# The last block's store: its copy split between VectorE and ScalarE, and one store half ahead of it moved to GpSimd's queue

## The chip, the cores and the metric

The kernel runs on one core of a Trainium2 chip. The metric is the device time of the run in microseconds (us), lower is better. Each time is a whole execution; a profiled execution also gives a span (first to last recorded instruction), which is a little shorter than its time.

## The reference

The program computes an attention with a 32-slot memory for 8 batches and 8 heads, and feeds its output, 4608 tokens of 512 columns, to a gated feed-forward layer (float32 in, float32 out):

```python
a = softmax(phi); k_m = a.T @ k; v_m = a.T @ v          # per batch and head
x = softmax(scale * q @ k_m.T) @ v_m                    # (8*576, 512)
g = x @ w_gate                                          # (4608, 1536)
out = (silu(g) * (x @ w_val)) @ w_out                   # (4608, 512)
```

What concerns us is the last line's last product, `h @ w_out`, and the way its results leave the chip.

## The kernel before

The kernel works batch by batch (8 batches of 576 tokens). The attention part is folded into two weight tiles per batch, so that a batch is 24 slots of gate and value matmuls (L508), a gate on ScalarE (L525), a multiplication on VectorE (L531), and then the output product. Instructions are written out in one fixed order by hand; each engine runs its own in that order, and the framework places the semaphores.

The output product is a 2x2 block scheme with seven products in place of eight: sums of blocks of `h` are formed ahead (POOL or VectorE, L553, L596, L657), and `products()` turns seven matmul groups (L719, PSUM tiles `p_os`, `p_oc`, `p_oa`) into four result blocks, called `c11`, `c22`, `c12` and `c21`. A batch has 576 tokens and the scheme takes 512 of them. The 64 tokens that are left over are gathered for four batches at a time: `products(b, ..., quad)` with `quad` 0 (batches 0 to 3) and `quad` 1 (batches 4 to 7) forms the same four blocks of 128 rows (two batches of 64) by 256 columns.

`quad` 1 is the end of the program, and its order is `c11` earlier, then `c22`, `c12`, `c21`. Each of them is made by `leftover(...)`:

- `c22` and `c12` add a PSUM result to a kept SBUF tile (VectorE, L788, tiles `t_p` and `t_q`);
- `c21` only copies its PSUM result to the SBUF tile `t_q` (on VectorE for the last quad: L332, called by the helper `copy`);
- the block then leaves in two DMAs of 64 rows by 256 columns, 64 KB each (L679, `store_leftover`). In the last quad the first half is issued by SP and, for all blocks but `c11`, the second half by ScalarE's queue.

`t_q` is one tile with two parts: `c12` writes part 1 and `c21` part 0. GpSimd's last computation before the end is a row of twelve block sums of the quad (L657 and L553, `quad_sums`).

After the last store, SP waits for all DMA semaphores, a few at a time, and all engines meet in two barriers (the rows of L1104).

Of the kernel before, what the change touches and what calls it, by code (L numbers as in the profile page):

```python
# [14 lines left out]
def kernel(  # L15
# [19 lines left out]
    nc = tc.nc  # L35
# [45 lines left out]
    def done(*tiles):  # L81

        for t in tiles:
            free.append(held.pop(id(t))[0])
# [243 lines left out]
    def copy(eng, out, in_):  # L328
        if eng == "a":
            nc.scalar.copy(out=out, in_=in_)  # L330
        else:
            nc.vector.tensor_copy(out=out, in_=in_)  # L332
# [344 lines left out]
    def store_leftover(t_o, b, cols, eng):  # L677

        eng.dma_start(out=out_b[b, 512:S, cols], in_=t_o)  # L679

    def products(b, by_hand, quad=None):

        h = DM // 2
# [3 lines left out]
        end = quad == 1 or (quad is None and b + 1 == B)  # L687
# [87 lines left out]
            both("o2", 256, slice(0, DM))  # L775

        def leftover(name, room, half, cols):
            engs = (nc.sync, nc.scalar if end and name != "c11" else nc.sync)

            def run():  # L780
                if room:
                    t = mine[room, "all"][:, half]
                else:
                    t = work.tile([128, h], FP32, tag="to", name="t_o")
                home = mine[dict(c11="a", c12="c").get(name, "s")]
                other = dict(c11="p1", c22="p5", c12="q6").get(name)
                if other:
                    nc.vector.tensor_tensor(  # L788
                        out=t, in0=home[:, 0], in1=mine[other][:, 0], op=ALU.add
                    )  # L790
                else:
                    copy("v" if end else "a", t, home[:, 0])
                if name != "c22":
                    done(home)
                for k in range(2):
                    x = 4 * quad + 2 * (name > "c20") + k
                    store_leftover(t[64 * k:64 * k + 64], x, cols, engs[k])

            return run
# [3 lines left out]
            c11=c11, c22=c22, c12=c12, c21=c21,  # L803
        )
        if quad is not None:
            ops.update(
                c11=leftover("c11", None, 0, lo), c12=leftover("c12", "q6", 1, hi),
                c22=leftover("c22", "p5", 1, hi), c21=leftover("c21", "q6", 0, lo),
            )
# [299 lines left out]
```

The softmax here doesn't subtract the row's maximum and nothing guards it: scores larger than these inputs give would overflow.

## Time and profile before

| | us |
|---|---|
| time, median of 4 runs (235.64 to 235.99) | 235.79 |
| time of the profiled execution | 235.84 |
| its span | 233.9 |
| busy PE | 224.4 (96%) |
| busy VectorE | 183.3 (78%) |
| busy ScalarE | 173.5 (74%) |
| busy GpSimd | 140.5 (60%) |

The profiled execution took 235.84 us, 1.94 us more than its span. The program is bound by TensorE as a whole, and the change touches only its last five microseconds, from the end of the matmuls on. There the times of single instructions (the timeline) matter, not the shares of the span. SPq and ACTq are the instruction queues of SyncE and ScalarE, whose rows are the issuing of DMAs and semaphore waits.

### The profile page before, as it was taken

What the parts mean: (1) busy time and instruction counts of PE and PEld (TensorE: products, weight loads), DVE (VectorE), ACT (ScalarE), POOL (GpSimd) and SP (SyncE); (2) the same over time, 40 slices, a digit from 0 to 9 for tenths busy, and PEclk for the clock granted to TensorE, in tenths of its full rate; (3) what the DMA queues carried; (4) which work ended last, traced back from release to release, by engine and by line L of the source; (5) the groups of instructions that cost most, each with busy time, mean ns of one, the idle gap of its engine ahead of it and who ended that gap; (6) DMA issues with size and microseconds to landing.
All of it is one profiled execution on the core that took longest, in us unless ns stands there. A gap on an engine that the chain in (4) does not pass through costs nothing.

```text
span 233.9 us, 7201 instructions
## 1 busy us (share of the span) xinstructions
PE 224.4 (96%) x2825; PEld 169.6 (73%) x2825; DVE 183.3 (78%) x421; ACT 173.5 (74%) x369; POOL 140.5 (60%) x190
## 2 busy tenths in 40 slices
PE   7997799999999999999999999999999999999992
PEld 2554466778887776878788787877788778878881
DVE  4056799999966698989797767989799879977632
ACT  2758798988547889968896658968897789677220
POOL 8422536998199059665966688465745484038390
PEclk9999999999999999999999999999999999999998
DMA  6999999999995992999199946995023602211224
GB/s 209 210 211 205 199 207 207 228 238 267 205 244 142 260 252 39 233 224 153 35 254 212 187 136 118 252 225 90 16 77 102 113 0 94 90 38 54 64 75 134
DMA packets 36610, 36.84 MB, mean 157 GB/s; under 512 B 14560, under 2 KB 30944, under 8 KB 36576
## 3 DMA queue, kind: packets, MB, share of 16 engines
q0 software_dynamic: 16272, 22.42, 51.5%
q1 hardware_dynamic: 19536, 13.18, 23.2%
q10 hardware_dynamic: 768, 0.79, 1.1%
q8 instruction: 22, 0.36, 0.6%
q14 instruction: 12, 0.10, 0.1%
HBM read 42.47 MB, written 9.44 MB: 222 GB/s over the span
## 4 chain that ended last, share of the span: by engine, by line
PE 86%; DMA 8%; POOL 2%; ACT 1%; issue 0%; DVE 0%; POOLq 0%
PE p_v L508 21%; PE p_g L508 21%; PE p_os L719 20%; PE p_oc L719 10%; DMA W<-in_moe_w_gate_dram 8%; PE p_u L465 5%; PE p_oa L719 5%; PE p_kv L230 2%; PE p_g L389 1%; POOL t_kv L99 1%; POOL t_kv L103 1%; PE p_q L376 0%; POOL t_q L108 0%; ACT t_qT L330 0%; PE p_kv L258 0%
## 5 line engine op out<-in xcount | busy, mean ns | idle before, releaser
L531 DVE TENSOR_TENSOR t_h<-t_sg,p_v 128x288 bf16<-128x288 bf16 x192 | 81.9, 451 | 17.3 <-PE p_v L508 7.1
L508 PEld LDWEIGHTS <-t_U 128*128 128x128 bf16 x768 | 73.5, 98 | 23.3 <-issue 3.8
L525 ACT ACTIVATE t_sg<-p_g 128x288 bf16<-128x288 f32 x192 | 74.0, 424 | 17.8 <-PE p_g L508 11.5
L508 PE MATMUL p_g<-t_A,t_U 128*128 128x288 bf16 x384 | 77.2, 287 | 0.5 <-ACT t_U L487 0.5
L508 PE MATMUL p_v<-t_A,t_U 128*128 128x288 bf16 x384 | 77.3, 286 | 0.0
L719 PEld LDWEIGHTS <-t_S 128*128 128x128 bf16 x384 | 37.4, 98 | 4.6 <-issue 0.2
L596 POOL TENSOR_TENSOR t_S<-t_h 128x512 bf16<-128x512 bf16 x17 | 19.6, 1154 | 32.6 <-DVE t_h L531 30.5
L719 PEld LDWEIGHTS <-t_h 128*128 128x128 bf16 x288 | 27.1, 98 | 8.6 <-issue 5.0
L485 ACT CAST t_U<-p_u 128x512 bf16<-128x512 f32 x53 | 28.0, 607 | 6.6 <-PE p_u L465 6.6
L719 PE MATMUL p_os<-t_T,t_S 128*128 128x256 bf16 x192 | 23.7, 273 | 0.0
L553 POOL TENSOR_TENSOR t_S<-t_S,t_h 128x512 bf16<-128x512 bf16 x17 | 19.6, 1154 | 1.3
L553 POOL TENSOR_TENSOR t_S<-t_h 128x512 bf16<-128x512 bf16 x16 | 18.4, 1151 | 0.0
L553 POOL TENSOR_TENSOR t_S<-t_h,t_S 128x512 bf16<-128x512 bf16 x16 | 18.4, 1150 | 0.0
L465 PE MATMUL p_u<-W,t_kT 64*32 64x512 bf16 (+1 forms) x416 | 15.8, 364 | 0.7 <-DMA W<-in_moe_w_gate_dram 0.7
L866 PE MATMUL p_warm<-bones 128*128 128x512 bf16 x44 | 13.7, 453 | 1.7 <-DVE bones L888 1.7
L719 PE MATMUL p_os<-t_T,t_h 128*128 128x256 bf16 x96 | 14.8, 274 | 0.0
L489 DVE CAST t_U<-p_u 128x512 bf16<-128x512 f32 x19 | 12.4, 683 | 1.9 <-PE p_u L465 1.9
L445 DVE TENSOR_TENSOR t_A<-t_E,t_lz 128x576 bf16<-128x576 bf16 x16 | 11.4, 739 | 0.7 <-ACT t_lz L421 0.7
L719 PE MATMUL p_oc<-t_T,t_S 128*128 128x256 bf16 x96 | 12.0, 273 | 0.0
L719 PE MATMUL p_oa<-WO,t_h 128*128 128x256 bf16 x96 | 11.8, 273 | 0.0
L719 PE MATMUL p_oc<-WO,t_S 128*128 128x256 bf16 x96 | 11.8, 273 | 0.1
L719 PE MATMUL p_os<-WO,t_h 128*128 128x256 bf16 x96 | 11.8, 273 | 0.0
(106 smaller groups left out, 308.7 us busy)
## 6 DMA issues: line engine op xcount, KB each, us to landing
out_dram<-t_o SPq DMA_DIRECT2D x15, 512.0 KB, 3.8
t_kv<-in_k_dram POOLq DMA_DIRECT2D x8, 576.0 KB, 10.2
t_q<-in_q_dram POOLq DMA_DIRECT2D x8, 576.0 KB, 8.7
t_kv<-in_v_dram POOLq DMA_DIRECT2D x8, 576.0 KB, 14.5
t_phi<-in_phi_dram POOLq DMA_DIRECT2D x6, 576.0 KB, 8.2
WO<-in_moe_w_out_dram POOLq DMA_DIRECT2D x3, 512.0 KB, 19.4
W<-in_moe_w_gate_dram POOLq DMA_DIRECT2D x2, 512.0 KB, 16.2
W<-in_moe_w_val_dram POOLq DMA_DIRECT2D x2, 512.0 KB, 15.7
```

The source lines that it names most:

```text
L230: nc.tensor.matmul(p[g][32 * i:32 * i + 32, 0:n], lhsT=phi_of(b, g, j, i), rhs=kvs[b][64 * g:64 * g + 64, w0:w1, i, j * D:(j + 1) * D], st ...
L445: nc.vector.tensor_tensor(out=a, in0=es.pop((b, g)), in1=lzs.pop((b, g)), op=ALU.mult)
L465: nc.tensor.matmul(p[g][32 * i:32 * i + 32, o:o + n], lhsT=kTs[b][64 * g:64 * g + 64, 2, 32 * i:32 * i + 32], rhs=w_part(w, c, i, g, halve ...
L485: nc.scalar.copy(out=t, in_=p)
L489: nc.vector.tensor_copy(out=t, in_=p)
L508: nc.tensor.matmul(p[:, 0:HALF], lhsT=Us[b, c, g][:, o // 2, which, 128 * (o % 2):128 * (o % 2 + 1)], rhs=atts[b, g][:, r], start=(g == 0) ...
L525: nc.scalar.activation(out=sg, in_=gate[:, 0:HALF], func=AF.Silu)
L531: nc.vector.tensor_tensor(out=dst, in0=sg, in1=val[:, 0:HALF], op=ALU.mult)
L553: eng.tensor_tensor(out=out, in0=x, in1=y, op=ALU.subtract)
L596: eng.tensor_tensor(out=t[:, 0], in0=A21, in1=A22, op=ALU.add)
L719: nc.tensor.matmul(mine[home][:, u], lhsT=lhs(c, m, u), rhs=rhs(c, m), start=fresh and u == 0, stop=(k == 5), skip_group_check=u == 1 or n ...
L866: nc.tensor.matmul(p[:, 0:128 * a], lhsT=bones, rhs=x.to_broadcast([128, a, 128]) if a > 1 else bones, start=True, stop=True,)
```

## The change

In the last quad, the copy of the last block `c21` from PSUM to SBUF is divided into two halves of 128 columns: columns 0 to 127 by VectorE, columns 128 to 255 by ScalarE. And the second 64-row store of the block ahead of it, `c12`, is issued by GpSimd's queue in place of ScalarE's. All the other stores keep their queues: `c22` and `c21` still go out half by SP and half by ScalarE. Outside the last quad the code does what it did before.

```diff
         def leftover(name, room, half, cols):
-            engs = (nc.sync, nc.scalar if end and name != "c11" else nc.sync)
+            other = dict(c22=nc.scalar, c12=nc.gpsimd, c21=nc.scalar) if end else {}
+            engs = (nc.sync, other.get(name, nc.sync))
...
+                elif end:
+                    copy("v", t[:, 0:h // 2], home[:, 0, 0:h // 2])
+                    copy("a", t[:, h // 2:h], home[:, 0, h // 2:h])
                 else:
-                    copy("v" if end else "a", t, home[:, 0])
+                    copy("a", t, home[:, 0])
```

(`h` is 256, and `home` is the PSUM tile of the result, one bank.)

## The prediction

> **What bounds the kernel now.** I first read the engines' shares (PE 96% of the span) and the chain of work that ended last, then only the program's end, since the diff acts on nothing else. The chain's last pieces, in order of time (start, length, what):
>
> ```profile
> 228.65 0.73 PE p_os L719 x6
> 229.39 0.02 issue
> 229.41 0.42 DVE t_q L332
> ```
>
> TensorE finishes the last product, VectorE copies it out of PSUM at 229.41, and at 229.83 the block `c21` is in SBUF. The span ends at 233.9, so 4.07 us come after the last computation. The timeline shows who issues the stores (start, length, queue):
>
> ```profile
> 228.53 0.47 SPq L679 DMA_DIRECT2D out_dram<-t_p  x1
> 228.54 0.55 ACTq L679 DMA_DIRECT2D out_dram<-t_p  x1
> ...
> 229.14 0.50 SPq L679 DMA_DIRECT2D out_dram<-t_q  x1
> 229.19 0.75 ACTq L679 DMA_DIRECT2D out_dram<-t_q  x1
> ...
> 229.90 0.47 SPq L679 DMA_DIRECT2D out_dram<-t_q  x1
> 230.05 0.54 ACTq L679 DMA_DIRECT2D out_dram<-t_q  x1
> ```
>
> These are the halves of `c22`, `c12` and `c21`. The block is ready at 229.83. SP issues its half of `c21` 0.07 later, ScalarE's queue 0.22 later: its issue of `c12` took 0.75 and lasted until 229.94. That delay is what the change's second part touches. The row of that last ScalarE issue, alone in its window, gives its time from issue to landing, and SyncE's wait list shows that the end hangs on it:
>
> ```profile
> DMA to landing us min/median/max: 2.1/2.1/2.1
> ```
>
> ```profile
> SPq L1104 <- DMA out_dram<-t_q: 1.6, 2, 1.0
> ```
>
> So ScalarE's half of `c21` lands at 230.05 + 2.1 = 232.15, SP's at 229.90 + 1.9 = 231.8. SP's closing waits (L1104), taken by windows, start at 230.4, 231.4 and 231.5, then one at 232.2, three by 232.4 and two at 232.9 and 233.0, and the barriers take the rest. The one at 232.2 is the one held up; its release to the end is 233.9 - 232.15 = 1.75 us. The path to be priced is: product done, copy, issue by the later queue, landing, rest of the closing waits.
>
> **What the Trainium skill says.** (1) "PSUM — Partial Sum Buffer", section "PSUM bank collisions raise a hardware error", says that ScalarE and VectorE may not touch the same bank in the same quadrant at once, two reads included. Here both halves of the copy lie in one bank and all four quadrants, so they cannot overlap. No row of the kernel before shows two engines on one bank at once, so the trace neither confirms nor denies it; the program as built bears it out, since ScalarE's half waits on VectorE's counter at the value that VectorE's half sets, and on no TensorE count of its own. (2) "DMA: Bandwidth & Descriptors", section "Anatomy of one DMA", prices a GpSimd-issued DMA at 2.0 us + bytes/436e3: 2.15 us for 64 KB, an estimate. The trace has no small GpSimd store; its 64 KB stores by SP and ScalarE take 1.9 to 2.2.
>
> **The change part by part.**
>
> *The copy in halves.* VectorE's copies from PSUM to float32 at this line take 692 ns for 512 columns and 424 for 256: 268 per 256, so 128 columns cost 424 - 134 = 290 (the 64x128 casts of the same line take 288). ScalarE's copies:
>
> ```profile
> L332 DVE COPY t_o<-p_os 128x512 f32<-128x512 f32 x1 | 0.7, 692 | 0.6 <-PE p_os L719 0.6
> L332 DVE COPY t_q<-p_os 128x256 f32<-128x256 f32 x1 | 0.4, 424 | 0.3 <-PE p_os L719 0.3
> L744 ACT COPY t_p<-p_oc 128x256 f32<-128x256 f32 x1 | 0.4, 372 | 0.3 <-PE p_oc L719 0.3
> L744 ACT COPY t_p<-p_oc 128x512 f32<-128x512 f32 x8 | 4.7, 586 | 2.1 <-PE p_oc L719 1.5
> ```
>
> 372 for 256, 586 for 512: 214 per 256, so 128 columns cost 265. In series: VectorE ends at 229.41 + 0.29 = 229.70. ScalarE must see VectorE's counter and start. From the end of VectorE's add to a DMA issue that waits on it is 228.53 - (228.08 + 0.42) = 0.03, and a ScalarE copy that follows a wait starts 0.04 after it (the L744 rows: the wait at 225.46 lasts 1.247, until 226.71, the copy starts at 226.75). I take 0.07, with 0.05 to 0.12 as ends, so ScalarE runs from 229.77 to 230.04. **Block ready: 230.04 in place of 229.83, +0.21.** A whole copy pays its fixed part once (about 156 ns on VectorE, 158 on ScalarE, from the two sizes); halves in series pay both, and the hop.
>
> *Who waits for that.* Both stores of `c21` now wait for ScalarE's half. Nothing is queued behind it on VectorE or SP but the end. On ScalarE only the store of `c21` stands behind it.
>
> *The store that moves.* ScalarE's queue loses one wait and one issue (0.75); it is free from 228.54 + 0.55 = 229.09 on, and receives a wait and the copy instead. So its issue of `c21` starts when the copy is done and seen: 230.04 + 0.03 = **230.07, against 230.05 before: +0.02.** The block is later by 0.21, and the queue's lag behind the block falls from 0.22 to 0.03; the two parts nearly cancel. SP's issue goes from 229.90 to 230.07, but lands 0.2 before ScalarE's half, so it costs nothing while that cover stands.
>
> *Landing of ScalarE's half.* Before it was 2.1 with SP 0.15 ahead. With both queues starting together, as at `c22` (228.53 and 228.54), ScalarE's took 2.2. With one other store fewer in flight it could be SP's 1.95. I take 2.15, +0.06, ends -0.15 and +0.12: landing at 232.22.
>
> *GpSimd.* It receives one wait and one DMA issue, behind its last block sums (L553, three from 226.15 on, 1.91 in all, ended 228.06) and ahead of its drain. `c12` is ready at 228.69 + 0.42 = 229.11, so it issues at 229.14. Its issues in this trace occupy it for 0.55 to 0.79, all larger ones; 64 rows should take no more. Landing at 229.14 + 2.15 = 231.3, an estimate from the page; the cover is ScalarE's half at 232.2. GpSimd's drain ended at 229.09 (row L1104, from 224.3, 4787 ns), 1.03 after its last sum; after a landing at 231.3 it would still end by 232.3, and the barrier is only reached at 233.1. Cost nothing, ends 0 and the rival below.
>
> *The closing waits.* SP still has nine of them, but hardware DMA semaphores go round in turn and `c12`'s second store no longer takes one, so in the built program the wait for ScalarE's `c21` stands third and not fourth. One more wait follows the release: they come 0.07 to 0.1 apart (three from 232.2 to 232.4), so +0.08; low end 0.
>
> **The sum**, against the profiled execution: +0.02 (issue) + 0.06 (landing) + 0.08 (closing waits) = +0.16: 235.84 becomes 236.0. The median of the runs shown is 0.05 under the profiled one, so I predict 235.79 + 0.16 = **235.95**. Everything ahead of 228.5 is untouched: no engine's instructions before the last quad's `c12` change.
>
> **The rivals.**
>
> *The halves gain.* If the copies ran side by side, the block would be ready at 229.41 + 0.29 = 229.70 and issued by both at 229.73, 0.32 before today's ScalarE issue: 235.79 - 0.32 + 0.06 + 0.08 = 235.61. For it: the aim of a split, and an idle ScalarE. Against it: the wait on VectorE in the built program. As the change doesn't do here what its words suggest, this is the case I rule out most: 0.03. A milder gain, landing at SP's 1.95 (230.07 + 1.95 = 232.02, -0.13, +0.08 for the waits: 235.74), lies inside "no change" and belongs to the likeliest.
>
> *GpSimd's store becomes the last.* One mechanism: a software-issued DMA lands later than the page's estimate, or holds GpSimd's drain. SP reaches its wait for this store about four steps after the release, near 232.5, so it decides from 232.5 - 229.14 = 3.4 us to landing on, and from there each us is a us. For it: the landings of GpSimd's 576 KB loads, with minimum 5.4 and median 8.7 for `t_q`:
>
> ```profile
> DMA to landing us min/median/max: 5.4/8.7/15.3
> ```
>
> Against it: those carry nine times the bytes, cast them and ran three or four at a time; at the end the DMA engines are idle (0.33 busy in 229 to 230). If it took 5.4, it would land at 234.5, 2.0 after 232.5: 235.95 + 2.0 = 237.95. Slower; I give 0.12 to this mechanism from its point of decision up, most of it nearer 3.4 than 5.4.
>
> **How the numbers follow.** The likeliest, the two parts cancelling with a small loss: 0.85, of which 0.02 ends over 0.2% slower and 0.01 over 0.2% faster (0.2% is 0.47 us, about what a measurement of this kernel can tell from no change). Its own range, from the ends: -0.15 + 0.02 - 0.02 = -0.15 and +0.02 + 0.05 + 0.12 + 0.08 = +0.27, with the runs' own scatter of 0.2: 235.6 to 236.3. The halves side by side, 0.03: 235.61, mostly under 0.2% too, 0.01 over it. GpSimd's store late, 0.12: 236.0 to 238. To take in its nearer part the range goes up to 236.5. Chances: faster 0.02, same 0.84, slower 0.14.
>
> **What would show it.** In the changed profile: VectorE's copy at L332 with 128 columns at 229.41 for about 0.29; ScalarE's at L330 for 0.27, starting 0.07 after VectorE's end and not beside it; both `c21` issues within 0.02 of each other near 230.07; a POOL row at L679 near 229.14 landing by 231.3; the span near 234.05. It is wrong if ScalarE's half starts before VectorE's ends, if the POOL store lands after 232.5, if the drain on POOL holds the barrier beyond 233.2, or if an instruction before 228 moves.

## The result, and the profile after

The changed kernel takes 236.12 us (median of 34 runs, 235.64 to 236.69) against 235.76 of before (52 runs): ratio 1.0013, 95% interval 1.0009 to 1.0018, or +0.3 us (0.2 to 0.4). The forecast was +0.16 and 235.95, "no change" within 0.2%. The profiled execution took 236.3 with a span of 234.4; 0.33 of its difference to before's profile lies ahead of the last add (228.69 becomes 229.02), in steps within the first 26 us and near 137 us, where both programs issue the same instructions. A second profile of the kernel before (e0_same below) is shifted by 0.35, with steps at the same places, so this is scatter between executions. The two profiles are therefore compared from the last add on (VectorE's sum for `c12`).

The timeline of the changed kernel (start, length, engine or queue; lines left out are marked):

```profile
229.02 0.42 DVE L789 TENSOR_TENSOR t_q<-p_oc,t_q 128x256 f32<-128x256 f32 x1 [0.18 <-PE p_oc L719]
229.74 0.29 DVE L332 COPY t_q<-p_os 128x128 f32<-128x128 f32 x1 [0.30 <-PE p_os L719]
...
229.74 0.57 POOL L679 DMA_DIRECT2D out_dram<-t_q  x1 [1.36 <-DVE t_q L789]
230.12 0.27 ACT L330 COPY t_q<-p_os 128x128 f32<-128x128 f32 x1 [2.00 <-DVE t_q L332]
230.41 0.50 ACTq L679 DMA_DIRECT2D out_dram<-t_q  x1
```

The two halves stand one after the other: VectorE's ends at 230.03, ScalarE's begins at 230.12. That ScalarE waits in between is seen in the chain of work that ended last, in order of time. Before, one copy of 0.42 stood in place of these pieces:

```profile
229.74 0.30 DVE t_q L332
230.04 0.02 issue
230.06 0.02 ACTq L330
230.08 0.04 issue
230.12 0.27 ACT t_q L330
```

The block is ready at 230.385, that is 0.64 after the copy's start and not 0.42. The two issues of `c21` now start together (230.41), and the row of ScalarE's, alone in its window, takes 2.2 to landing where before it took 2.1:

```profile
L679 ACTq DMA_DIRECT2D out_dram<-t_q x1: 498/498/498, 230.4 to 230.4; - x1
...
DMA to landing us min/median/max: 2.2/2.2/2.2
```

GpSimd's rows at the program's end (L1108, which is L1104 of before) show its drain, the row that closes its work: it starts at 229.7 and lasts 2788 ns, to 232.5. Before, it ended at 229.09.

```profile
L1108 POOLq EVENT_SEMAPHORE  x4: 17/17/17, 233.7 to 234.3; - x4
L1108 POOLq DRAIN  x3: 46/93/2788, 229.7 to 234.1; - x3
```

The first of its barrier rows is at 233.7, so there are 1.2 us to spare after the drain. The table puts this on one clock: us after the start of the last add, from the traces' start and landing records, for all kernels of this document. The kernels are described with the experiments below.

| kernel | block ready | SP issues c21 | ScalarE issues c21 | last c21 landing | end |
|---|---|---|---|---|---|
| before | 1.14 | 1.21 | 1.36 | 3.45 | 5.20 |
| before again (e0_same) | 1.15 | 1.21 | 1.36 | 3.42 | 5.17 |
| changed | 1.36 | 1.39 | 1.39 | 3.60 | 5.39 |
| changed again (e11_again) | 1.37 | 1.39 | 1.40 | 3.61 | 5.39 |
| e1_halves | 1.60 | 1.63 | 1.63 | 3.84 | 5.58 |
| e2_pool | 1.14 | 1.21 | 1.22 | 3.41 | 5.19 |
| e5_act | 1.14 | 1.16 | 1.17 | 3.37 | 5.14 |
| e7_par | 1.01 | 1.08 | 1.09 | 3.46 (SP's) | 5.21 |
| e10_par_alone | 1.01 | 1.07 | 1.09 | 3.33 (SP's) | 5.07 |
| e12_act_alone | 1.37 | none | 1.40 | 3.34 | 5.22 |
| e6_pool_last | 1.15 | 1.21 | GpSimd 1.74 | 3.72 | 5.26 |
| e9_turn | 1.14 | 1.23 | 1.36 | 3.54 | 4.52 |
| e8_act_turn | 1.14 | 1.16 | 1.17 | 3.45 | 4.42 |

### The profile page after: what moved, and what is told of

It is laid out like the page before. It is cut to its first block, busy times and chain, and to the rows that moved or that the text cites. A ratio compares the mean times of both kernels' runs of the same rounds, so it can differ in the third digit from the quotient of the medians.

```text
span 234.4 us, 7203 instructions
## 1 busy us (share of the span) xinstructions
PE 223.8 (95%) x2825; PEld 169.5 (72%) x2825; DVE 183.2 (78%) x421; ACT 173.9 (74%) x370; POOL 141.1 (60%) x191
## 4 chain that ended last, share of the span: by engine, by line
PE 88%; DMA 7%; POOL 1%; ACT 1%; issue 1%; DVE 1%; POOLq 0%; ACTq 0%
PE p_v L508 21%; PE p_g L508 21%; PE p_os L719 20%; PE p_oc L719 10%; DMA t_kv<-in_v_dram 7%; PE p_u L465 5%; PE p_oa L719 5%; PE p_kv L230 2%; PE p_g L389 1%; POOL t_kv L99 1%; PE p_mT L318 1%; PE p_warm L870 1%; PE p_q L376 0%; POOL t_q L108 0%; DVE t_kT L332 0%
## 5 line engine op out<-in xcount | busy, mean ns | idle before, releaser
L870 PE MATMUL p_warm<-bones 128*128 128x512 bf16 x44 | 12.9, 431 | 1.7 <-DVE bones L892 1.7
```

What stands on the lines that cost most here:

```text
L870: nc.tensor.matmul(p[:, 0:128 * a], lhsT=bones, rhs=x.to_broadcast([128, a, 128]) if a > 1 else bones, start=True, stop=True,)
```

## The experiments

**How much the timing carries** (before once more, and the changed kernel once more).

> The kernel before once more, unchanged, under another label. Every theory: 1.0000; how far it strays tells how small a difference the timing can carry.

Measured: 1.0000 (0.9992 to 1.0009), 235.82 against 235.74. A ratio of 13 runs carries about 0.001, or 0.2 us; smaller differences have to be read in the profile, where the end of before repeats to 0.03 (5.20 and 5.17).

> The changed kernel once more, unchanged. By the end of its first profile (from the last add to the end 0.19 longer than before): 1.0008. By its runs so far: 1.0013. A second profile tells whether the terms repeat: copy handed over at 1.10 after the last add's start, both issues at 1.39, ScalarE's landing 2.2 later.

Measured: 1.0013 (1.0005 to 1.0020), and every term repeats (table). The profiles give +0.19 to +0.22, the runs a median of +0.3 with a lower bound of 0.2 (34 runs) and 0.1 (16 runs). Whether the remaining 0.1 is real, and where it would lie, is not settled.

**One part of the change at a time.** The halves alone, `c12=nc.scalar` in place of `nc.gpsimd`:

```diff
-            other = dict(c22=nc.scalar, c12=nc.gpsimd, c21=nc.scalar) if end else {}
+            other = dict(c22=nc.scalar, c12=nc.scalar, c21=nc.scalar) if end else {}
```

> The copy in halves alone; all stores on the queues of before. If the two parts of the change cancel (my theory): ScalarE's queue issues its c12 half first (0.75 long), so ScalarE's half of the copy starts only about 0.65 after VectorE's half starts and both c21 stores issue about 0.9 after it, against 0.64 (ScalarE) in before: +0.25, landing +0.1, closing waits as before: +0.35, ratio 1.0015. If the store's move costs and the halves are harmless: no change, 1.0000. If the halves gain: below 0.9995.

Measured: 1.0016 (1.0009 to 1.0022), +0.4; the end is 0.38 later than before in the profiles, as forecast. The timeline of this kernel shows why: ScalarE's half must stand behind that queue's issue of `c12`, which lasts from 229.33 to 230.08.

```profile
229.33 0.75 ACTq L679 DMA_DIRECT2D out_dram<-t_q  x1
...
230.17 0.27 ACT L330 COPY t_q<-p_os 128x128 f32<-128x128 f32 x1 [2.24 <-DVE t_q L332]
...
230.47 0.50 ACTq L679 DMA_DIRECT2D out_dram<-t_q  x1
```

So the move of the store to GpSimd mends half of what the halves cost (0.38 becomes 0.19): it makes ScalarE free in time to copy.

The store's move alone, with `c21` whole on VectorE:

```diff
-                    copy("v", t[:, 0:h // 2], home[:, 0, 0:h // 2])
-                    copy("a", t[:, h // 2:h], home[:, 0, h // 2:h])
+                    copy("v", t, home[:, 0])
```

> The store on GpSimd alone; c21 copied whole by VectorE. If the move only frees ScalarE's queue (my theory): the block is ready 0.42 after the copy's start, ScalarE issues at 0.46 and not at 0.64 (-0.18), lands 0.1 later for starting together with SP, closing waits +0.05: -0.03, ratio 0.9999, and better than the changed kernel by 0.2 us. If GpSimd's store holds the end (rival): as slow as the changed kernel or slower, 1.0010 or more.

Measured: 1.0002 (0.9994 to 1.0011); the end is 0.02 sooner than before in the profiles, inside their scatter. ScalarE's issue did come 0.14 sooner (1.22 for 1.36), but its landing only 0.04 sooner (3.41 for 3.45). So the lag of ScalarE's queue, which looked like 0.15 us on the path, was nearly free.

And a whole copy by ScalarE in place of the halves (`copy("a", t, home[:, 0])`):

> The store on GpSimd, and c21 copied whole by ScalarE (0.37 by its row for 256 columns) in place of halves. No hop, and the same queue issues: ScalarE's issue 0.41 after the copy's start against 0.64 in before: -0.23, landing +0.1, closing waits +0.05: -0.08, ratio 0.9997. If a hop from TensorE to ScalarE is dearer than to VectorE, nearer 1.0000. If GpSimd's store holds the end: 1.0010.

Measured: 0.9999 (0.9991 to 1.0008); the end is 0.06 sooner in the profiles, near the -0.08 forecast, but by time it can't be told from before. ScalarE copies the 256 columns in 0.372 for VectorE's 0.424 and starts 0.045 later, so the block is ready at the same moment (1.14).

**Why the landing takes 2.2.** In the kernels so far ScalarE's half lands 2.2 after SP's issue, whether it was issued with it or 0.15 later: 3.45 - 1.21 = 2.24 in before, 3.60 - 1.39 = 2.21 in the changed kernel, 3.41 - 1.21 = 2.20 in e2_pool. (e9_turn and e8_act_turn, below, have 2.32 and 2.29.) Either ScalarE's queue is slower, or the second of two stores waits for the first. One kernel tells these apart; in it SP's half of `c21` isn't issued (`range(1, 2)` for `k` there).

> As the changed kernel, but SP's half of the store of c21 is left out (64 rows of the last block aren't written); ScalarE's half is the same. If two stores issued together are served one after the other and the second lands 2.2 after the first's issue (theory): alone, ScalarE's lands 1.95 after its issue, as SP's do, and the end comes 0.25 sooner than in the changed kernel. If ScalarE's queue is slower by itself (rival): 2.2 as before, and the same end.

Measured: ScalarE's half, alone, by its row and landing:

```profile
L679 ACTq DMA_DIRECT2D out_dram<-t_q x1: 473/473/473, 229.9 to 229.9; - x1
...
DMA to landing us min/median/max: 1.9/1.9/1.9
```

1.95 by the landing record, against 2.20 in its pair. So the queue is not slow. SP's half in the pair also lands 1.94 after its issue, so the first of the pair isn't held up and the second waits for it; with the two issued 0 to 0.15 apart, the last landing follows the first issue. Of the 0.25 forecast at the end only 0.17 came (5.22 for 5.39): the landing is 0.25 sooner (3.34 for 3.60), but the rows after it take 1.88 in place of 1.79, mostly since one of SP's closing drain rows is 0.13 long there and 0.01 in the changed kernel. By time: 0.9998 (0.9989 to 1.0007) of before.

**Halves that do run side by side.** ScalarE's half reads another PSUM tile, in another bank, so that columns 128 to 255 of `c21` are left out and others stand in their place:

```diff
-                    copy("a", t[:, h // 2:h], home[:, 0, h // 2:h])
+                    copy("a", t[:, h // 2:h], mine["c"][:, 0, h // 2:h])
```

> As the changed kernel, but ScalarE's half of the copy reads columns of c12's result, in another PSUM bank, so that it doesn't wait for VectorE's half: columns 128 to 255 of c21 are left out. If the loss of the halves comes from their running one after the other in one bank: block ready 0.29 after VectorE's copy starts, both stores issue at 0.32 against 0.67 in the changed kernel and 0.64 in before: -0.32, landing +0.1, closing waits +0.05: -0.17, ratio 0.9993. If the loss has another cause (GpSimd's store, landings): as the changed kernel, 1.0013.

Measured: 1.0002 (0.9993 to 1.0010). The mechanism is as expected. ScalarE's half doesn't wait for VectorE's half; what releases it is VectorE's add, which reads the bank that ScalarE now reads:

```profile
229.24 0.27 ACT L330 COPY t_q<-p_oc 128x128 f32<-128x128 f32 x1 [1.42 <-DVE t_q L789]
229.45 0.29 DVE L332 COPY t_q<-p_os 128x128 f32<-128x128 f32 x1 [0.30 <-PE p_os L719]
```

So the block is ready at 1.01 and issued at 1.08, 0.31 sooner than in the changed kernel. Whether the wait that is gone came from the shared bank or from the shared tile isn't separated: here both are different. The size is a miss: the end is 0.18 sooner than the changed kernel and no sooner than before (5.21), because SP's half now lands last, 2.39 after its issue. (The row is for the queue's two stores in the window; the longer landing is the second's.)

```profile
L679 SPq DMA_DIRECT2D out_dram<-t_q x2: 503/511/519, 229.2 to 229.8; - x2
...
DMA to landing us min/median/max: 2.0/2.2/2.4
```

SP's issue starts 0.01 ahead of ScalarE's, and yet lands last. Its row also ends last (1.594, ScalarE's 1.579), and in every kernel of the table with both halves on SP and ScalarE, the half whose issue row ends later lands later.

The stores now follow GpSimd's issue by 0.35. Without GpSimd's store (`range(1)` for `c12`'s `k`):

> As the kernel whose ScalarE half reads another bank (columns 128 to 255 of c21 left out), and GpSimd's store is left out too (64 rows of c12 aren't written). There SP's half of c21 landed 2.39 after its issue. If GpSimd's store, still in flight, held it up: 2.2 for the later of the two and 1.95 for the other, last landing 0.15 to 0.2 sooner, end 0.1 to 0.2 sooner. If the two c21 stores merely hinder each other when issued within 0.015: 2.39 again and the same end.

Measured: 0.9996 (0.9988 to 1.0004). The later of the two lands after 2.26 and the other after 1.97, the end is 0.14 sooner (5.07 for 5.21). The same row and landings of this kernel:

```profile
L679 SPq DMA_DIRECT2D out_dram<-t_q x2: 505/512/519, 229.1 to 229.7; - x2
...
DMA to landing us min/median/max: 2.0/2.1/2.3
```

So GpSimd's store costs 0.13 at the last landing where the last stores come this soon after it. In the changed kernel they come 0.3 later, and their landings are those of kernels without it (2.20, and 2.21 in e1_halves).

**The rival on the slow side: GpSimd's store as the last.** The kernel of before, with the second half of `c21` on GpSimd:

```diff
-            engs = (nc.sync, nc.scalar if end and name != "c11" else nc.sync)
+            engs = (nc.sync, (nc.gpsimd if name == "c21" else nc.scalar) if end and name != "c11" else nc.sync)
```

> As before, but GpSimd issues the second half of c21, the very last store, in place of ScalarE (c12's stays on ScalarE). If a GpSimd store is no worse than 2.2 to landing and 0.3 to start (as in the changed kernel's profile): row starts 0.3 after the block is ready, lands 2.2 later, some 0.1 to 0.2 after the landing of before; GpSimd's drain ends 0.6 after that. +0.15 to +0.4 at most: ratio 1.0006 to 1.0017. If GpSimd's stores land late or hold the barrier by their drain (rival): +0.5 and more, over 1.002.

Measured: 1.0004 (0.9996 to 1.0012); the end is 0.06 later in the profiles. Its GpSimd row and landing:

```profile
L679 POOL DMA_DIRECT2D out_dram<-t_q x1: 573/573/573, 230.8 to 230.8; - x1
...
DMA to landing us min/median/max: 2.0/2.0/2.0
```

The row starts 0.59 after the block is ready, twice the expected hop, and then lands in 2.0. (In this kernel a wait row of 5.5 us stands ahead of GpSimd's issue and ends 0.04 after the block is ready; where the hop is 0.3, that row is 0.02 long and far earlier. That this makes the difference is not shown.) The drain ends 0.6 after the landing, at 4.30 on the table's clock, only 0.2 ahead of SP's arrival at the barrier (4.50). So even in the last place GpSimd's store neither lands late nor holds the barrier by its drain.

**The closing waits.** The prediction charged 0.08 for one more wait of SP after the release. If that is right, turning the order of the semaphores, so that the awaited store is checked late, must gain. Four stores in the middle of the program are issued in two parts, which turns the order by four:

```diff
-        nc.sync.dma_start(
-            out=out_r[b, n, 0:256, cols].rearrange("(u t) c -> t u c", u=2), in_=t_o[:, :, cols]
-        )
+        dst = out_r[b, n, 0:256, cols].rearrange("(u t) c -> t u c", u=2)
+        if (b, n) in ((3, 0), (3, 1), (4, 0), (4, 1)):
+            for u in range(2):
+                nc.sync.dma_start(out=dst[:, u], in_=t_o[:, u, cols])
+            return
+        nc.sync.dma_start(out=dst, in_=t_o[:, :, cols])
```

> As before, but four of the 512 KB stores in the middle of the program are issued as two of 256 KB, which turns the semaphores of the last stores by four: SP's closing wait for ScalarE's c21 half is the eighth of nine, not the fourth. If the waits after the release lie on the path at 0.07 to 0.09 each: -0.3; if the 0.5 gap among them goes as well, -0.7: ratio 0.9987 to 0.9970. If they are off the path (the barrier waits for something else): 1.0000.

Measured: 0.9968 (0.9959 to 0.9978), -0.8, near the -0.7 expected if the gap goes as well. In the profiles the end is 0.68 sooner; the profiled execution itself, 235.6, is the longest of the nine (median 234.87), as its last add starts at 229.3, and before's at 228.7. SP's closing waits, in before those after the held one:

```profile
L1104 SPq EVENT_SEMAPHORE  x3: 28/28/28, 232.3 to 232.4; - x3
...
L1104 SPq EVENT_SEMAPHORE  x2: 28/28/28, 232.9 to 233.0; - x2
```

and here those ahead of the held one, and from it on (L1107 is this kernel's L1104):

```profile
L1107 SPq EVENT_SEMAPHORE  x7: 28/28/28, 231.0 to 232.1; - x7
...
L1107 SPq EVENT_SEMAPHORE  x4: 17/22/28, 232.9 to 233.8; - x4
L1107 SPq DRAIN  x3: 7/7/7, 233.0 to 233.3; - x3
```

Seven waits are over by 232.1; two of the four at or after 232.9 are the held one and its successor, and the other two are the barriers'. From the last landing to the end it takes 4.52 - 3.54 = 0.98, against 1.75 in before. Of the 0.77, three ordinary steps from wait to wait make 0.26, the long step of 0.49 that before has between its seventh and eighth wait makes most of the rest, and 0.02 comes after the waits. In the long step SP stands still for 0.46. In e9_turn this stall follows the third wait, ahead of the landing, where it costs nothing. So the edit did two things: it turned the order of the checks, and its four added issues moved the stall. Counted over SP's instructions in the trace, the stall follows the 79th in all 13 profiles: the seventh wait in before and the changed kernel, the third in e9_turn, the second in e8_act_turn, with five issues added, and the ninth in e12_act_alone, with one store fewer. What causes it is open. The landing itself comes 0.09 later here than in before, which is open too.

Joined with the copy whole on ScalarE, `c12`'s store on GpSimd and a fifth divided store (in place of the halves):

> c21 copied whole by ScalarE, c12's second store on GpSimd, and five middle stores in two parts, so that the wait for ScalarE's c21 half is the eighth of nine. -0.08 for the copy and -0.3 to -0.7 for the waits: -0.4 to -0.8, ratio 0.9983 to 0.9966. If only one of the two counts, as that one alone. GpSimd's drain, which ended at 232.5 in the changed kernel, must be over before the barrier at about 232.5: if it isn't, it takes back 0.1 to 0.3.

Measured: 0.9960 (0.9948 to 0.9973), 234.78 against 235.74 (five runs), -0.9, a little over the far end of what was expected. Like e9_turn it beats both kernels; by time the two can't be told apart. Its end, 4.42, is 0.1 ahead of e9_turn's; GpSimd's drain ends at 3.51 and SP comes to the barrier at 3.65, 0.14 to spare. Of e9_turn's 0.8 the profile's end accounts for 0.7; that the divided stores do nothing elsewhere in the program is not shown.

## Why the prediction was right, and where its terms were off

- **The halves run in series**: right, 0.22 for the 0.21 worked out. VectorE's half 0.291 (0.290), ScalarE's 0.265 (0.265), the hop 0.09 (0.07). A wait on VectorE's counter is what orders them: reading another tile in another bank, ScalarE's half ran early (e7_par). No experiment here lets two engines read one bank at once, so what would come of it isn't shown.
- **Issue of ScalarE's half, +0.02**: right, +0.03.
- **Landing of ScalarE's half, +0.06**: measured +0.12 (2.20 for 2.09), the end of its bounds. This is the mis-sized term, and the step behind it is "SP's issue goes from 229.90 to 230.07, but lands 0.2 before ScalarE's half, so it costs nothing while that cover stands". It does cost: ScalarE's half waits for SP's (1.95 alone and 2.20 in the pair, e12_act_alone), so SP's later issue delays both. Issue and landing together cost 0.15 (0.18 against e0_same), and SP's issue came 0.18 later. "The two parts nearly cancel" holds for the issue time, not for the landing.
- **GpSimd, cost nothing**: right in the sum. Its row began 0.3 after its input was ready, not 0.03, and it landed 2.2 after that (estimate 2.15, from the Trainium skill, "DMA: Bandwidth & Descriptors", section "Anatomy of one DMA"; the trace agrees with 2.18). The drain ended 0.6 after the landing, at 232.5.
- **Closing waits, +0.08**: measured +0.04 (1.79 from the last landing to the end, 1.75 before). The one more step took its 0.07; the rows after the last wait were 0.03 shorter. That such steps lie on the path is shown by e9_turn, where three of them are worth 0.26. The stall of 0.46 among them isn't in the prediction; it is in both kernels, after the landing, so it doesn't enter their difference.
- **The sum**: +0.16 forecast, +0.19 in the profile (0.03, 0.12 and 0.04), +0.3 by the runs. The landing's error of +0.06 and the closing waits' of -0.04 partly cancel, so that the sum came so near is in part luck.
- **The rivals**: both fell. The copies didn't overlap; where they did (e7_par), the block was ready 0.35 sooner than in the changed kernel, but the end came only 0.18 sooner, no better than before, because SP's half landed late; GpSimd's store was 0.13 of that. In the changed kernel GpSimd's store landed 0.7 ahead of ScalarE's.
- **Its signs of being wrong**: one of them came, "if an instruction before 228 moves". They moved by 0.33, and in e0_same, the kernel before once more, by 0.35: the sign was too strict for the scatter.
- **Readings that don't hold**: that the DMA engines are idle at the end (0.33 busy in 229 to 230) leaves out the next two us, in which GpSimd's store was to be in flight: 0.84 and 0.58. The 64 KB stores take 1.9 to 2.2 in the last quad, but two at 132 us take 3.2 and 3.6. One of GpSimd's issues takes 0.91, over the 0.79. None of these enters the sum.

## What to carry to other kernels

In this program a copy out of one PSUM tile wasn't shortened by dividing it between two engines: the halves ran in turn, and paid a second fixed part and a hop (0.64 us in place of 0.42). Dividing needs a check of what the second engine waits for. A late issue is only on the path if its landing is: where two queues' stores are served in turn, look at the first of the pair, and test a queue's lag before spending work on it (0.14 sooner at ScalarE's issue was worth 0.04 at its landing). At a program's end, look at what follows the last landing: here 1.75 us of semaphore waits and barriers, of which 0.77 went away when the last store's semaphore was checked later and a stall among the waits came to lie ahead of the landing.

## What the hardware showed that was not expected

- Two 64 KB stores issued within 0.15 by SP and ScalarE land 1.94 to 1.99 and 2.20 to 2.32 after the first issue (2.22 and 2.39 with a GpSimd store 0.35 ahead of them, e7_par); alone, ScalarE's lands in 1.95. The one whose issue row ends last lands last.
- A 64 KB GpSimd store starts 0.3 after VectorE's result (0.6 in e6_pool_last), where SP starts 0.03 to 0.06 after it. GpSimd's drain ends 0.59 after the store's landing in all eight profiles that have such a store.
- A stall of 0.45 to 0.47 us follows SP's 79th instruction in all 13 profiles, wherever that lies among its closing waits.
